# One fused attention and feed-forward kernel: the order of two early loads, chunk 1's queries and the second piece of `w_in`

## The chip, the cores and the metric

The kernel runs on one core of a Trainium2 chip. The core has TensorE (PE: matrix products; weight loads are listed apart as PEld), VectorE (DVE), ScalarE (ACT), GpSimd (POOL) and SyncE (SP, which here only issues transfers). Transfers between the chip's main memory and the on-chip memory run on 16 DMA engines that all queues share. The metric is the device time of one execution in microseconds (us). Six runs of the kernel before gave a median of 259.49 us, from 259.06 to 260.13.

## The reference, cut to what matters

Two blocks follow each other. The first is an attention with polynomial sketches: queries and keys are projected by two 8x32 matrices `S1` and `S2`, the 8x8 outer product of both projections gives 64 features, and the keys' features are summed up against the values.

```python
# q, k, v: (4, 4, 1088, 32);  S1, S2: (8, 32)
def phi(x):
    a = np.einsum('rd,bhsd->bhsr', S1, x)
    b = np.einsum('rd,bhsd->bhsr', S2, x)
    return np.einsum('bhsi,bhsj->bhsij', a, b).reshape(*x.shape[:-1], r * r)
q_p, k_p = (phi(q), phi(k))
kv = np.einsum('bhsf,bhsd->bhfd', k_p, v)
z = np.sum(k_p, axis=2)
num = np.einsum('bhsf,bhfd->bhsd', q_p, kv)
den = np.einsum('bhsf,bhf->bhs', q_p, z)[..., None] + 1e-06
attn_out = (num / den).astype(np.float32)

# x: attn_out as (4352, 128);  w_in: (128, 2048);  w_out: (2048, 128)
h = x @ w_in
g = 0.5 * h * (1.0 + erf(h * inv_sqrt2))
return (g @ w_out).astype(np.float32)
```

`w_in`, `w_out`, `S1` and `S2` arrive with 64-bit elements; the kernel loads both 32-bit words of each and rounds them to 32-bit floats on the chip.

## The kernel before, in words

The 1088 tokens of each of the 4 batches are cut into two chunks of 512 and a remainder of 64; the remainders of all batches form a ninth chunk. So chunk 0 and chunk 1 are the halves of batch 0. For each chunk the kernel makes `xT`, the attention output with its 128 channels on the partitions, then 16 hidden tiles (line 721, a product of `xT` with 128 columns of `w_in`, and Gelu at line 728), and sums them into the output with `w_out` (lines 807 and 858).

The weights are cut into five pieces of 256, 256, 512, 512 and 512 columns (`CUTS`, line 85), each a tile of its own: `w_in_sb[0]` serves hidden tiles 0 and 1, `w_in_sb[1]` hidden tiles 2 and 3. A piece lands in a raw tile (the pieces of 256 in tiles called `small`, those of 512 in tiles called `block`). The class `Rounding` (line 243) turns it into floats in steps: `low_words` (line 260, ScalarE), `exponent_fields` and `mantissa_fields` (lines 268 and 273, VectorE), `exponents` (line 279, ScalarE), `mantissas` (line 287, VectorE), `signs` (line 292, VectorE) and `product` (line 297, VectorE or POOL).

Every engine runs its instructions in the order of the text: at the end of the kernel a loop chains them (line 1219). SP's order is therefore that of the calls to the `load_` functions. It begins with batch 0's keys (line 192), chunk 0's queries (line 193), batch 0's values (line 195) and three remainders (line 197); then come `w_in`'s first piece, chunk 1's queries and `w_in`'s second piece (lines 198 to 200). The next entry on SP is the first piece of `w_out`, in `load_w_out` (line 175). It is gated: POOL writes one element of its landing tile (line 180), and the load waits for that write. POOL does it after the product of `w_in`'s first piece (lines 933 and 934). All remaining loads follow in `load_rest` (line 202).

How the loads in question are used, in the order of the text:

- Chunk 0's queries are turned by VectorE (line 528). Its features, the sums over keys and values (lines 426 and 432) and the rounding of `w_in`'s first piece follow.
- `query_turn(1, ...)` at line 928 turns chunk 1's queries with four TensorE transposes (line 333). ScalarE copies the result to `qT` at line 937; `expand_products(1)` (line 543) reads it.
- `w_in[1].low_words()` and `w_in[1].exponent_fields()` (lines 938 and 939) are the first readers of the second piece. Its other steps stand at lines 945, 951 and 955 to 957.
- Between them TensorE computes chunk 0's numerators by token (line 656, called at line 943), `expand_products(1)`, the transposes of chunk 0's attention output (line 694) and the first hidden tile (line 737). The other hidden tiles of chunk 0 follow at line 721.

At the very start, and once before the sketches, `keep_busy` (line 890) fills TensorE with products of zeros.

Of the kernel before, what the change touches and what calls it, by code (L numbers as in the profile page):

```python
# [16 lines left out]
def kernel(  # L17
# [97 lines left out]
    def load_q(n):  # L115
        at = n % NCH * CW
        if n < NCH:
            sp.dma_start(out=q_sb[n], in_=q[0, :, at:at + CW, :].rearrange("h (p j) d -> p h j d", j=JC))
            return
        for h in range(H):  # L120
            sp.dma_start(out=q_sb[n][h * 32:(h + 1) * 32].rearrange("t x j d -> t (x j d)"),
                         in_=q[n // NCH, h, at:at + CW, :].rearrange("(t n) d -> t (n d)", t=32))
# [8 lines left out]
    def load_rem(n, b):  # L131
        sp.dma_start(out=rem[n][b // 2 * REM:(b // 2 + 1) * REM, b % 2],
                     in_=src_of[n][b, :, MAIN:S, :].rearrange("h p d -> p h d"))
# [13 lines left out]
    def landing(dst, wide):  # L147

        if wide:
            rows, n = dst.shape  # L150
            if n == 512:

                if not half_block:
                    half_block.append(block())
                    r = half_block[0][:, 0:2]
                else:
                    r = half_block.pop()[:, 2:4]
                raw[dst.name] = r.rearrange("p a b -> p (a b)").rearrange("p (n two) -> p n two", two=2)
            elif n == 256:
                raw[dst.name] = small(U32).rearrange("p (n two) -> p n two", two=2)  # L160
            else:
                raw[dst.name] = big.tile([rows, n, 2], U32, name=f"raw_{dst.name}")
            return raw[dst.name].rearrange("p n two -> p (n two)")
        return dst

    def words(a):

        return (a, 1) if a.dtype == FP else (a.bitcast(U32), 2)

    def load_w_in(i):  # L170
        src, e = words(moe_w_in)
        c0, c1 = pieces[i]
        sp.dma_start(out=landing(w_in_sb[i], e == 2), in_=src[:, c0 * e:c1 * e])
# [22 lines left out]
    for n, b in (("k", 0), ("k", 2), ("v", 0)):  # L196
        load_rem(n, b)
    load_w_in(0)
    load_q(1)
    load_w_in(1)  # L200

    def load_rest():

# [1051 lines left out]
```

## Time and profile before

| what | value |
|---|---|
| median of six runs | 259.49 us (259.06 to 260.13) |
| the profiled execution's own time | 259.88 us |
| its span, first to last instruction | 258.1 us |
| granted TensorE clock over the span | 0.998 |
| TensorE matmul busy | 253.4 us, 98% of the span |
| VectorE, ScalarE, POOL busy | 151.1, 115.2, 164.1 us |
| read from and written to main memory | 10.88 MB, 2.23 MB |

The profile is of one execution, with times from the start of the span. "Busy" counts the time in which an engine has an instruction in execution; TensorE's matmuls overlap, and their ends are modelled, so that the start of one is firmer than its end. The chain that ended last is followed back from the last instruction, at each step to what released it; "issue" in it is time in which an engine waited for nothing that the profile shows. A DMA's time to landing runs from the start of its issue to the last of its 16 completion signals. The queues of kind "instruction" carry the program's own code.

### The profile page before, as it was taken

Reading aid. Unit: us, or ns where it says so; the run is one execution under the profiler, and the core shown is the slowest. Engines: PE = TensorE matmul, PEld = TensorE weight load, DVE = VectorE, ACT = ScalarE, POOL = GpSimd, SP = SyncE. Lnnn points to the kernel's source line nnn. Section 1 sums busy time; section 2 is a strip of 40 time slices with the busy share of each in tenths; the row PEclk is TensorE's granted clock in tenths of the full one; section 3 lists DMA queues with packets and bytes.
Section 4 is the critical chain, followed back from the end, with each engine's and each line's share of the span. In section 5 each row is a group of like instructions: output and inputs, shape, how many; then the busy total and the mean of one; then the engine's idle time right before and its main releaser. Section 6 shows DMA issues by size and latency. Waiting matters only on the chain.

```text
span 258.1 us, 5770 instructions
## 1 busy us (share of the span) xinstructions
PE 253.4 (98%) x2335; PEld 135.2 (52%) x2335; DVE 151.1 (59%) x313; ACT 115.2 (45%) x224; POOL 164.1 (64%) x173
## 2 busy tenths in 40 slices
PE   8899999999999999999999999999999999999995
PEld 7756444345444545544444455455444444445794
DVE  2886888969699997590187986399307000700330
ACT  4665777443626333443335332533444334433442
POOL 3504006799968778487758775787758777877300
PEclk9999999999999999999999999999999999999999
DMA  7489748810000101102000002000200200020020
GB/s 208 136 238 366 179 104 203 216 47 10 3 0 12 31 2 20 23 6 38 3 0 3 0 9 38 0 1 3 41 3 4 39 0 1 7 36 0 3 41 20
DMA packets 29594, 13.48 MB, mean 52 GB/s; under 512 B 21888, under 2 KB 27776, under 8 KB 29568
## 3 DMA queue, kind: packets, MB, share of 16 engines
q1 hardware_dynamic: 29392, 13.05, 20.4%
q8 instruction: 18, 0.29, 0.5%
q10 hardware_dynamic: 176, 0.07, 0.1%
q14 instruction: 8, 0.07, 0.1%
HBM read 10.88 MB, written 2.23 MB: 51 GB/s over the span
## 4 chain that ended last, share of the span: by engine, by line
PE 98%; issue 0%; ACT 0%
PE h_ps L721 45%; PE o_ps L807 33%; PE o_ps L858 5%; PE w_ps L855 3%; PE w_ps L437 1%; PE w_ps L578 1%; PE w_ps L633 1%; PE w_ps L890 1%; PE w_ps L543 1%; PE o_ps L426 1%; PE h_ps L737 1%; PE w_ps L978 1%; PE w_ps L656 0%; PE w_ps L333 0%; PE h_ps L333 0%
## 5 line engine op out<-in xcount | busy, mean ns | idle before, releaser
L721 PE MATMUL h_ps<-xT,w_in 128*64 128x512 f32 (+3 forms) x514 | 137.0, 576 | 0.0
L728 ACT ACTIVATE block<-h_ps 128x512 f32<-128x512 f32 (+1 forms) x128 | 73.1, 571 | 117.3 <-PE h_ps L721 115.3
L721 PEld LDWEIGHTS h_ps<-xT,w_in 128*64 128x64 f32 (+1 forms) x514 | 41.8, 142 | 30.6 <-issue 11.6
L807 PE MATMUL o_ps<-block,w_out 128*64 128x256 f32 x224 | 57.5, 379 | 0.0
L772 POOL TENSOR_TENSOR bits_low<-block 128x512 f32<-128x512 f32 x28 | 35.9, 1283 | 27.7 <-ACT block L728 27.7
L807 PEld LDWEIGHTS o_ps<-block,w_out 128*64 128x64 f32 x224 | 30.5, 137 | 38.1 <-issue 27.6
L773 POOL TENSOR_TENSOR bits_a<-block 128x512 f32<-128x512 f32 x28 | 35.8, 1278 | 11.9 <-ACT block L728 11.9
L822 DVE COPY sums<-o_ps 64x256 f32<-64x256 f32 x8 | 3.3, 417 | 60.7 <-PE o_ps L807 60.7
L774 POOL TENSOR_TENSOR bits_e<-bits_a,block 128x512 f32<-128x512 f32 x28 | 36.1, 1289 | 2.2
L775 POOL TENSOR_TENSOR bits_m<-block,bits_e 128x512 f32<-128x512 f32 x28 | 35.9, 1280 | 2.2
L807 PE MATMUL o_ps<-bits_a,small 128*64 128x256 f32 x112 | 28.8, 379 | 0.0
L807 PE MATMUL o_ps<-bits_low,small 128*64 128x256 f32 x112 | 28.8, 379 | 0.0
L807 PE MATMUL o_ps<-block,small 128*64 128x256 f32 x112 | 28.8, 379 | 0.0
L807 PE MATMUL o_ps<-bits_m,w_out 128*64 128x256 f32 x112 | 28.7, 379 | 0.0
L807 PEld LDWEIGHTS o_ps<-block,small 128*64 128x64 f32 x112 | 15.2, 137 | 17.9 <-issue 10.8
L807 PE MATMUL o_ps<-bits_e,small 128*64 128x256 f32 x112 | 17.0, 383 | 0.0
L858 PE MATMUL o_ps<-g,w_out 128*128 128x512 f32 (+1 forms) x34 | 16.5, 572 | 0.0
L807 PEld LDWEIGHTS o_ps<-bits_m,w_out 128*64 128x64 f32 x112 | 15.3, 137 | 0.0
L807 PEld LDWEIGHTS o_ps<-bits_a,small 128*64 128x64 f32 x112 | 15.2, 137 | 0.0
L807 PEld LDWEIGHTS o_ps<-bits_low,small 128*64 128x64 f32 x112 | 15.2, 137 | 0.0
L590 DVE STREAM_TRANSPOSE w_ps<-w_ps 128x512 f32<-128x512 f32 (+1 forms) x7 | 4.8, 688 | 17.0 <-ACT xT L644 12.7
L807 PEld LDWEIGHTS o_ps<-bits_e,small 128*64 128x64 f32 x112 | 7.6, 137 | 10.6 <-issue 8.8
(195 smaller groups left out, 304.1 us busy)
## 6 DMA issues: line engine op xcount, KB each, us to landing
block<-in_moe_w_in_dram SPq DMA_DIRECT2D x3, 512.0 KB, 7.6
block<-in_moe_w_out_dram SPq DMA_DIRECT2D x3, 512.0 KB, 11.3
k<-in_k_dram SPq DMA_DIRECT2D x12, 128.0 KB, 2.8
v<-in_v_dram SPq DMA_DIRECT2D x12, 128.0 KB, 3.3
q<-in_q_dram SPq DMA_DIRECT2D x24, 64.0 KB, 2.3
out_dram<-oT SPq DMA_DIRECT2D x21, 64.0 KB, 2.2
k<-in_k_dram SPq DMA_DIRECT2D x2, 256.0 KB, 3.3
q<-in_q_dram SPq DMA_DIRECT2D x2, 256.0 KB, 4.1
```

The source lines that it names most:

```text
L426: pe.matmul(ps[c * F:(c + 1) * F, r * 2 * D:r * 2 * D + C], lhsT=flat(k_p[0, r][:, t, c * 4 + ch * 2 + one]), rhs=v_aug[r][:, c, i, :C], s ...
L590: dve.transpose(out=tok, in_=ps[:, :, :H2])
L721: pe.matmul(ps[rows, :W], lhsT=w[:, rows], rhs=xT[n][:, :W], start=True, stop=True)
L728: act.activation(out=g_of[n, fi][:, :W], in_=ps[:, :W], func=ACT.Gelu)
L772: pool.tensor_sub(out=s[3], in0=a11, in1=a21)
L773: pool.tensor_add(out=s[1], in0=a21, in1=a22)
L774: pool.tensor_sub(out=s[2], in0=s[1], in1=a11)
L775: pool.tensor_sub(out=s[4], in0=a12, in1=s[2])
L807: pe.matmul(acc[n][bank][half * 64:(half + 1) * 64, col:col + HW], lhsT=fixed, rhs=moving, start=opens and e == 0 and name in "4715", stop ...
L822: dve.tensor_copy(out=N[lo, 0, one], in_=a0[lo, one])
L855: pe.matmul(o_of[n][i][:, :128], lhsT=g[:, i * 128:(i + 1) * 128], rhs=w_tile(w_out_sb, fi), start=first, stop=final)
L858: pe.matmul(o_of[n][:, cols], lhsT=w_tile(w_out_sb, fi), rhs=g[:, cols], start=first, stop=final)
```

## The change

The second piece of `w_in` is loaded ahead of chunk 1's queries, and not behind them. Nothing else is touched; the readers of both stand where they stood.

```diff
@@ -196,8 +196,8 @@
     for n, b in (("k", 0), ("k", 2), ("v", 0)):
         load_rem(n, b)
     load_w_in(0)
+    load_w_in(1)
     load_q(1)
-    load_w_in(1)
 
     def load_rest():
```

The two functions called, with `n` and `i` both 1:

```python
    def load_q(n):
        at = n % NCH * CW
        if n < NCH:
            sp.dma_start(out=q_sb[n], in_=q[0, :, at:at + CW, :].rearrange("h (p j) d -> p h j d", j=JC))
            return
...
    def load_w_in(i):
        src, e = words(moe_w_in)
        c0, c1 = pieces[i]
        sp.dma_start(out=landing(w_in_sb[i], e == 2), in_=src[:, c0 * e:c1 * e])
```

Each moves 256 KB: the queries as 512 rows of 512 bytes, the piece of `w_in` as 128 rows of 2,048 bytes.

## The prediction

> **What bounds the kernel now.** I read the page first, to see which engine carries the span, and in it the chain that ended last.
>
> ```profile
> span 258.1 us, 5770 instructions
> PE 253.4 (98%) x2335; PEld 135.2 (52%) x2335; DVE 151.1 (59%) x313; ACT 115.2 (45%) x224; POOL 164.1 (64%) x173
> PE 98%; issue 0%; ACT 0%
> ```
>
> TensorE is the chain from end to end. A change counts only if it opens or closes a gap between two of its instructions, or shortens them. So I next read the chain in order of time for the first 30 us, where both moved loads are used (start, length, what).
>
> ```profile
> 10.61 0.35 PE o_ps L432 x8
> 10.96 0.59 PE w_ps L333 x4
> 11.55 0.48 PE h_ps L656 x23
> 12.03 0.71 issue
> 12.74 0.32 PE h_ps L656 x9
> ```
>
> The four L333 pieces at 10.96 turn chunk 1's queries; they follow the sums before them without a gap. One line later is the only long gap of the start: 0.71 us at 12.03, in the middle of the chunk 0 numerators, put down to "issue" and to no semaphore. Third, the sync engine's timeline (start, length, queue and line, load), since the change is made there.
>
> ```profile
> 5.48 0.60 SPq L173 DMA_DIRECT2D small<-in_moe_w_in_dram  x1
> 6.13 0.43 SPq L118 DMA_DIRECT2D q<-in_q_dram  x1
> 6.61 0.50 SPq L173 DMA_DIRECT2D small<-in_moe_w_in_dram  x1
> 12.52 0.88 SPq L181 DMA_DIRECT2D small<-in_moe_w_out_dram  x2
> ```
>
> These are w_in's first piece, chunk 1's queries, w_in's second piece, and the gated loads behind them. Fourth, the two lines of the kernel by themselves, in the windows that hold only the second query load and only the second w_in load: issue to landing, the queries first; then the wait instruction that TensorE's sequencer executes before the turn.
>
> ```profile
> DMA to landing us min/median/max: 4.0/4.0/4.0
> ...
> DMA to landing us min/median/max: 4.3/4.3/4.3
> ...
> L333 PEldq EVENT_SEMAPHORE  x1: 51/51/51, 10.6 to 10.6; - x1
> ```
>
> So the queries land at 6.13 + 4.0 = 10.1 and w_in's second piece at 6.61 + 4.3 = 10.9. The wait at 10.6 ends at once; the list of waits has no line of TensorE on that load. Fifth, who reads the second piece, and what follows the turned queries (timelines of VectorE, ScalarE and TensorE).
>
> ```profile
> 11.58 0.29 DVE L268 TENSOR_SCALAR bits_e<-small 128x256 uint32<-128x256 uint32 x1
> ...
> 11.59 0.59 ACT L937 COPY qT<-w_ps 128x512 f32<-128x512 f32 x1 [0.35 <-PE w_ps L333]
> 12.07 0.43 ACT L260 ACTIVATE bits_low<-small 128x256 f32<-128x256 uint32 x1
> ...
> 13.46 1.12 PE L543 MATMUL w_ps<-qT,Srep 32*64 32x256 f32 x32
> ```
>
> None of these waits for the piece. Last, the DMA view from 10.4 to 10.6 us, which holds the end of all early loads: the columns are packets, MB and share of 16 engines.
>
> ```profile
> q8 instruction: 1, 0.02, 30.0%
> q1 hardware_dynamic: 1, 0.00, 0.3%
> ```
>
> One data packet ends the early loads, and one 16 KB packet of instructions starts there. 30% of 16 engines over 0.2 us is 0.96 us of one DMA engine. The same view from 10.6 to 13 us starts no packet at all. I read the 0.71 us gap as TensorE waiting for that block of code: it is in a group of 32 equal instructions, no semaphore ends it, and it is the first gap after the block arrives.
>
> **The change, part by part.**
>
> Removed and added: nothing. Two load instructions change places on the SP queue.
>
> The SP queue: w_in's second piece, 0.50 us of issue, passes the queries' 0.43 us. It is issued at 6.1 instead of 6.6, the queries at 6.1 + 0.5 = 6.6 instead of 6.1. The next instruction on SP, the gated load, goes at 12.52 after a wait of 5.4 us for POOL's memset; both issues are over by 7.1 either way. The memset follows POOL's product at 11.74, which waits for VectorE's signs at 11.24, made from the first piece, whose place is unchanged. So nothing behind on SP moves, and POOL's and ScalarE's own queues are passed by nothing: 0.
>
> w_in's second piece comes sooner. In the queries' old place it lands near 10.1 to 10.4 instead of 10.9. VectorE reads it first at 11.58, straight after the work in front of it in its order, ScalarE at 12.07: it had 0.7 us to spare already. TensorE needs it rounded at about 17.3 (third hidden tile), behind VectorE instructions that run without waiting for a load. Gain: 0. A gain is excluded because no reader waits.
>
> The queries come later. Both loads are 256 KB, so what is ahead of the last byte is the same in either order; I take for the queries the landing that the load in third place has now, 10.9. From below it is 6.61 + 4.0 = 10.6, if the queries keep their own time to landing; then nothing waits. From above, the block of code, which now starts when the data are through, gets in front of the last query packets on its DMA engine: 10.9 + 0.96 = 11.9. The middle value is the one nearest to the rows, because the code packet follows the last data packet in this trace and the number of packets ahead of it does not change.
>
> What that does to TensorE: its first L333 weight load starts at 10.89. A landing at 10.9 and a start just after it make a wait of about 0.1 us, at 11.0 (an estimate: the chunk 0 queries landed at 1.75 + 4.2 = 5.95, and VectorE began on them at 6.00). From below 0, from above 11.9 + 0.1 - 10.9 = 1.1 us. Behind the waiting instruction on TensorE stand the rest of the turn (0.59 us) and the numerators (0.48 us up to the gap). Those who wait for the turn: ScalarE's copy, 11.59 to 12.18, then at about 12.3; behind it the second piece's low words, 12.07 to about 12.2, not read before 15.9. TensorE uses the copy at 13.46, so 1.2 us are spare.
>
> The cover: the 0.1 us push the 23 numerators to end at 12.13 instead of 12.03, and the gap shrinks from 0.71 to 0.6. It ends at 12.74 as long as the code block leaves when it does now, and that packet starts at 10.5 behind the same bytes in either order. Path: +0.1 - 0.1 = 0. If that cover were gone the cost would be the whole wait, 0.1 and at most 1.1 us; with the cover the upper end is 1.1 - 0.71 = 0.4 us.
>
> [...]
>
> **Sum.** SP 0, second piece 0, queries +0.1, gap -0.1: 0.0 us. The profiled execution took 259.88 us, 1.78 outside its span; it lies 0.39 above the median of 259.49 of the six runs, and the change moves nothing that would carry that difference. I predict the median, rounded: 259.5 us. 0.2%, 0.52 us, is about what a measurement of this kernel can tell from no change.
>
> **Rivals.**
>
> Slower: the wait for the queries comes to lie on the path without its cover. Place: the four L333 turns at 10.89. The mechanism is the gap at 12.03 sliding along with the work before it. For it: the gap is labelled only "issue", and my reading of it as code is an inference. Against: no reason is visible why it should slide, since its packet starts at 10.5, before the wait. Price: the whole wait, 0.1 to 1.1 us, middle 0.6: 260.1 us, at most 260.6. It decides from a wait of 0.52 us, that is, from a landing of the queries at about 11.3.
>
> Faster: the code block overtakes the query packets, and the gap goes while the queries are not late. For it: the queries' many small rows now come last, and a packet that slips between them would start before 10.5. Against: on its DMA engine it occupies 0.96 us, by which the queries are then late, so the 0.71 us gained at 12.03 are lost at 10.9. Both would have to be true. Price: up to -0.71, 258.8 us.
>
> No effect by another road: the loads share the DMA engines so closely that both land as before. For it: issues 0.5 us apart and landings 0.8 apart. Price 0, 259.5 us; it ends with the forecast.
>
> Later stall: the turned queries reach TensorE late at 13.46. Against: 1.2 us spare against 0.1; even the upper end of 1.1 fits. 259.5 us.
>
> **How the numbers follow.** Forecast with the two rivals that end on it, path unchanged or moved within 0.52 us: 0.70. Slower rival: 0.22, of which I let all count as slower. Faster rival: 0.08. The range covers the forecast's own spread, 259.1 to 260.1 as the runs before lie, and reaches up to 260.4, over most of the slower rival, and down to 258.9, short of the faster one's end.
>
> **What would show it.** Right: w_in's second piece issued before the queries near 6.1; the queries landing near 10.9; the first L333 of chunk 1 at 10.9 to 11.1; the gap in L656 shortened to about 0.6 and ending near 12.7; the rest of the chain at its old times. Wrong: a line of TensorE waiting for the query load longer than 0.5 us; the gap ending later than 12.9, or gone; the instruction packet starting at another time than 10.5; the first L737 away from 15.3. The prediction fails if the gap is not tied to that packet, or if the order changes when the packet leaves.

## The result, and the profile after

The kernel after takes 259.86 us (median of 36 runs, 259.13 to 262.07), the kernel before 259.39 us (median of 74 runs). The ratio is 1.0019 with a 95% interval of 1.0011 to 1.0027: slower by 0.47 us, just within the 0.2% that the prediction set as its bound, but clear of no change. The profiled execution after took 259.90 us with a span of 258.1 us, the same span as that of the profiled execution before. So the two profiles shown first do not contain the difference; further executions were needed.

The page of the kernel after: its span, the engines' busy time, and the shares of the chain that ended last.

```profile
span 258.1 us, 5770 instructions
PE 253.3 (98%) x2335; PEld 135.6 (53%) x2335; DVE 151.1 (59%) x313; ACT 115.1 (45%) x224; POOL 164.0 (64%) x173
PE 94%; SPq 2%; DMA 2%; issue 0%; ACT 0%
```

The instructions are the same. What is new is 2% of DMA in a chain that was all TensorE. The chain in order of time (start, length, what) shows where:

```profile
6.12 0.43 SPq L173
6.55 0.04 issue
6.60 5.12 DMA q<-in_q_dram
11.71 0.14 issue
11.85 0.63 PE w_ps L333 x4
12.48 0.60 PE h_ps L656 x32
13.08 0.47 PE o_ps L656 x32
```

The order on SP is as the change says: `w_in`'s second piece at 6.12, chunk 1's queries at 6.60. But the queries take 5.1 us and land at 11.71, and TensorE cannot turn them before 11.85, where before it had started at 10.96 in this chain. And the 0.71 us gap at 12.03 is gone: the 32 numerators run in one piece, and the next products begin at 13.08, against 13.06 before. A wait of 0.8 us has come and a gap of 0.7 us has gone, in this pair of executions. The list of waits after, from 5 to 25 us (who waited for what: us in total, times, longest):

```profile
PE w_ps L333 <- DMA q<-in_q_dram: 0.8, 1, 0.8
ACT bits_low L260 <- DMA small<-in_moe_w_in_dram: 0.4, 1, 0.4
```

The second line is the first piece of `w_in`, which lands at 10.35; TensorE does not wait for it in this execution. The DMA view after, from 8.8 to 8.9 us, shows what has changed ahead of both (packets, MB, share of 16 engines):

```profile
q8 instruction: 1, 0.02, 82.5%
q1 hardware_dynamic: 19, 0.02, 59.4%
```

TensorE's 16 KB block of code leaves here, at 8.85 us, in the middle of the data, where it left at 10.48 in the profile before, behind all of them. (That queue q8 carries TensorE's code is my reading: the page of before gives it 18 packets and 0.29 MB, and TensorE 4,670 matmuls and weight loads, some 260 for each packet.) The trace gives each of a load's 16 completion signals. Of the queries' signals after, eleven come by 10.26, the other five between 10.51 and 11.71.

The trace also has the start and length of each packet, but not its engine. Where one packet starts as another ends and the rest follow without a break, I take them to be on one engine. By this the queries behind the code block run from 10.16 to 11.33. But a second engine, which has rows of `w_in`'s second piece until 10.67, runs its queries until 11.44. So in this execution the block is one of two causes of the late landing, and without it the queries would have been about as late.

### The profile page after: what moved, and what is told of

It reads as the page before. It is cut to its first block, busy times and chain, and to the rows that moved or that the text cites. A ratio compares the mean times of both kernels' runs of the same rounds, so it can differ in the third digit from the quotient of the medians.

```text
span 258.1 us, 5770 instructions
## 1 busy us (share of the span) xinstructions
PE 253.3 (98%) x2335; PEld 135.6 (53%) x2335; DVE 151.1 (59%) x313; ACT 115.1 (45%) x224; POOL 164.0 (64%) x173
## 4 chain that ended last, share of the span: by engine, by line
PE 94%; SPq 2%; DMA 2%; issue 0%; ACT 0%
PE h_ps L721 45%; PE o_ps L807 33%; PE o_ps L858 5%; PE w_ps L855 3%; DMA q<-in_q_dram 2%; PE w_ps L437 1%; PE w_ps L578 1%; PE w_ps L633 1%; PE h_ps L737 1%; SPq L132 1%; SPq L100 1%; PE w_ps L978 1%; PE w_ps L656 0%; PE w_ps L543 0%; SPq L173 0%; PE w_ps L333 0%
## 5 line engine op out<-in xcount | busy, mean ns | idle before, releaser
L773 POOL TENSOR_TENSOR bits_a<-block 128x512 f32<-128x512 f32 x28 | 35.7, 1276 | 12.0 <-ACT block L728 11.9
L807 PEld LDWEIGHTS o_ps<-bits_e,small 128*64 128x64 f32 x112 | 7.7, 137 | 10.6 <-issue 8.8
```

Source lines behind the costliest of these rows:

```text
L773: pool.tensor_add(out=s[1], in0=a21, in1=a22)
L807: pe.matmul(acc[n][bank][half * 64:(half + 1) * 64, col:col + HW], lhsT=fixed, rhs=moving, start=opens and e == 0 and name in "4715", stop ...
```

## The experiments

Fourteen executions were profiled in all. I tell two theories apart. A: the order of the two loads decides when the code block leaves, so that each order has its own profile. B: the block leaves early or late by the execution, and in either order it gets in front of whichever load stands third on its DMA engine; in before that load is one with time to spare, in after it is the one that TensorE waits for.

### Both kernels once more: look_before, look_after

Edit: none. `look_before` is the kernel before, `look_after` the kernel after.

> The kernel before, unchanged, looked at once more. Two theories. Theory A (order): in the order of before the block of code leaves behind both loads, near 10.5 us, and TensorE has the gap of about 0.7 us at 12.0; in the order of after it leaves in front of the queries, near 8.9, the gap is gone, and the queries land near 11.7. By A this look repeats the first: code at 10.4 to 10.6, a gap of 0.6 to 0.8 us in L656, no wait at L333. Theory B (chance): when the code leaves differs from execution to execution, whatever the order of the two loads. By B this look may as well show the code near 9 us, no gap at 12.0 and the first L333 at 10.9 to 11.1; then before is usually faster than its first profile by the gap.

> The kernel after, unchanged, once more, timed against before. Both theories expect the time at 1.001 to 1.003 of before. A: the profile repeats itself, with the code near 8.9 us, a wait of TensorE of 0.8 to 0.9 us for the query load and no gap at 12.0. B: the code may leave near 10.5; then the queries land near 10.9, the first L333 stands near 11.0, and the gap of 0.6 us is there.

Measured: `look_before` 258.9 us, span 257.1. `look_after` 259.8 us, 1.0017 of before (1.0002 to 1.0031), span 258.2. The chain of `look_before` around the place:

```profile
10.54 0.35 PE o_ps L432 x8
10.89 0.59 PE w_ps L333 x4
11.48 0.60 PE h_ps L656 x32
12.08 0.47 PE o_ps L656 x32
12.55 1.05 PE w_ps L543 x32
```

No gap: all 32 numerators run through, and the next products begin at 12.08, 1 us earlier than in the first profile of before. Its DMA view from 8 to 10.4 us has the instruction packet that the first profile of before had at 10.48 (start 8.79 by the trace):

```profile
q1 hardware_dynamic: 658, 0.52, 65.7%
q8 instruction: 1, 0.02, 2.9%
```

Here the third load, `w_in`'s second piece, pays for it: it lands at 6.6 + 4.8 = 11.4, and nobody waits for it. In `look_after` the third load is the queries; of their 16 signals fifteen come by 10.45, the last at 11.81:

```profile
11.81 0.14 issue
11.95 0.63 PE w_ps L333 x4
12.58 0.60 PE h_ps L656 x32
```

In this trace the first row behind the block starts at 10.28, as the block ends at 10.29, and from 10.4 on the packets follow one another on that engine alone: this landing is the block's doing.

Theory A falls: before has the early block too. These two executions fit theory B, and the account below limits it. The gap that I had counted on as cover is not in every execution.

### Chunk 1's queries first: q_first

```diff
-    load_w_in(0)
     load_q(1)
+    load_w_in(0)
     load_w_in(1)
```

> Chunk 1's queries are loaded ahead of both pieces of w_in. If the loss of after is TensorE's wait for the queries, this order has no such wait (queries landing near 9.5): time at or below before, 0.998 to 1.000, with the gap at 12.0 of 0 to 0.8 us depending on when the code leaves. w_in's first piece lands about 0.7 us later than in before, near 10.1 to 10.4; VectorE reads it at 10.3, so at most 0.3 us of VectorE's spare time is used. If the loss of after were something else than the queries' landing (the two w_in pieces back to back, for instance, which this order has too), this one would lose about 0.2% as well.

Measured: 0.9998 of before (0.9988 to 1.0007). The interval lies below that of after, 1.0011 to 1.0027. The two pieces of `w_in` stand back to back here too, without the loss of after, so that neighbourhood is not the cause. The queries come in time; in their place the first piece is late, at 10.6, and ScalarE waits for it (list of waits of `q_first`):

```profile
ACT bits_low L260 <- DMA small<-in_moe_w_in_dram: 0.7, 1, 0.7
```

By the table below this costs 0.2 us, since the sums' copy stands behind that instruction on ScalarE and TensorE's numerators wait for it. The expectation put the first piece at 10.1 to 10.4 and the cost at spare time of VectorE alone; it did not see ScalarE's order.

### The second piece out of the early queue: w1_gated

```diff
-    def load_w_in(i):
+    def load_w_in(i, gated=False):
...
-        sp.dma_start(out=landing(w_in_sb[i], e == 2), in_=src[:, c0 * e:c1 * e])
+        to = landing(w_in_sb[i], e == 2)
+        if gated:
+            pool.memset(to[0:1, 0:1], 0)
+        sp.dma_start(out=to, in_=src[:, c0 * e:c1 * e])
...
     load_w_in(0)
     load_q(1)
-    load_w_in(1)
...
     widen_v(0)
+    load_w_in(1, gated=True)
```

> w_in's second piece is taken out of the early queue: its load waits for a one-element write of POOL behind the first widening of the values, near 7.4 us, and so is issued near 7.5 and not at 6.6, behind the queries. If the DMA backlog ahead of the code block makes the gap at 12.0, the block leaves about 0.6 us earlier than 10.5 (eight rows of 2 KB at 0.08 us fewer ahead of it on its DMA engine), and the gap shrinks to 0.1 or goes; the queries still land near 10.1 and TensorE does not wait for them: 0.997 to 0.999 of before. If the gap is not tied to that packet it stays at about 0.7 us, and the time is that of before, 0.999 to 1.001. The second piece then lands near 11.5 to 12, still before ScalarE's and VectorE's next use at 13.

Measured: 1.0001 of before (0.9991 to 1.0011). Its profile has the code at 8.90, the queries at 10.3, the second piece at 11.4 and no gap and no wait between the sums and the first hidden tile. The gain of 0.1 to 0.3% that I expected did not come, and by theory B little of it could: the late block with its long gap, which it guards against, is in one of five executions of before.

### More executions, and less or more in front of the queries: look_before2, look_after2, w1_half, q_gated

`look_before2` and `look_after2` are before and after, unchanged. The edit of `w1_half`, against after:

```diff
-        sp.dma_start(out=landing(w_in_sb[i], e == 2), in_=src[:, c0 * e:c1 * e])
+        to = landing(w_in_sb[i], e == 2)
+        m = (c1 - c0) * e // (2 if i == 1 else 1)
+        sp.dma_start(out=to[:, :m], in_=src[:, c0 * e:c0 * e + m])
...
     for t in v_aug:
         dve.memset(t[:, :, :, D:C], 1.0)
+    dve.memset(raw[w_in_sb[1].name].rearrange("p n two -> p (n two)")[:, 256:], 0)
```

The edit of `q_gated`, against after:

```diff
     load_w_in(0)
     load_w_in(1)
-    load_q(1)
...
     widen_v(0)
+    pool.memset(q_sb[1][0:1, 0, 0, 0:1], 0.0)
+    load_q(1)
```

> A third look at before, to see how often the gap at 12.0 us is there. Of two looks one had it (code block leaving at 10.5, span 258.1) and one had not (code at 8.8, no gap, span 257.1). If the code usually leaves early, this look has the code near 9, the first L333 at 10.9 to 11.2, no gap of over 0.3 us after it, and a span of 257.1 to 257.5. The span should be the start of the first L737 plus 242.7 us, as in all six profiles so far.

> A third look at after. In two of two the code left near 9 and the queries landed at 11.7 and 11.8. If that is the usual course, this look shows them at 11.2 to 11.9 and a wait of TensorE of 0.4 to 1.0 us; span again the start of the first L737 plus 242.7. If the wait were an accident of those two executions, the queries land near 10.9 and the wait is 0.1.

> The order of after, but w_in's second piece loads only its first 128 columns; VectorE fills the other half of the landing tile with zeros at the start, so hidden tile 3 is left without its weights. The queries then have four rows of 2 KB fewer ahead of them on each DMA engine, 0.32 us at 0.08 each. If the queries' landing at 11.7 is the data ahead plus the code block on one DMA engine, they land near 11.4 and TensorE waits about 0.6 instead of 0.9 us; time 0.9985 to 1.001 of before, 0.3 us below after. If bytes ahead do not matter, 11.7 and the time of after, 1.002.

> The order of after, with the queries held back further: their load waits for a one-element write of POOL behind the first widening of the values, near 7.4 us, and is issued 0.8 to 1.0 us later than in after. If the queries' landing sets TensorE's start at L333 one for one, and they are behind the code block already, they land 0.0 to 0.5 us later (11.7 to 12.3), TensorE waits 0.9 to 1.5 us and the time is 1.002 to 1.005 of before. If the late landing in after were only the later issue, the wait would grow by the whole 0.8 to 1.0 us, to 1.7 to 2.0, and the time to 1.006. If the wait at L333 did not pass through to the end, the time stays at 1.002 with a longer wait.

Measured: `look_before2` 259.27 us, `look_after2` 259.82 us, `w1_half` 1.0013 of before (1.0003 to 1.0023), `q_gated` 1.0020 (1.0008 to 1.0032).

`look_after2` repeats the late queries, at 11.63. `look_before2` shows that the order of before is not free either. Its second piece lands at 12.05, and the list of waits of that execution has

```profile
DVE bits_e L268 <- DMA small<-in_moe_w_in_dram: 0.5, 1, 0.5
```

VectorE stands at the exponent fields of that piece while the numerators it should divide are ready, and TensorE later stands idle for 0.17 us until VectorE has divided them (line 694).

That is not the whole loss of 0.25 us in this execution. TensorE's lines for the 32 numerators, first in `look_before`, then in `look_before2`:

```profile
11.41 0.67 PE L656 MATMUL h_ps<-kz,q_pT 64*64 64x33 f32 x32
```

```profile
11.44 0.85 PE L656 MATMUL h_ps<-kz,q_pT 64*64 64x33 f32 x32
```

The 0.18 us more lie between the 23rd and the 24th matmul, where the first profile of before has its gap. The 24th starts 1.30 us after the end of the code packet in the first profile of before and 1.40 us after it here. In the other twelve executions it starts 1.7 us or more after that end, and there is no gap. Without VectorE's wait `look_before2` would still lose some 0.17 us (an estimate: 0.17 us of idle time less in front of line 694, and 0.33 us from there to the first hidden tile, as in `look_before`).

`w1_half` puts the queries at 6.6 + 4.5 = 11.1, 0.5 to 0.7 us earlier than the first three executions of after (I expected 0.3). TensorE does not wait for them, the turn following the last sums at 11.30, and yet the time did not come down to the 0.9985 to 1.001 that I expected. It lies between before and after, but the interval holds after's 1.0019 too, so only the landing is shown, and that in one execution. That it is the smaller load which moves it is not shown either: the last query packet ends at 10.29, and the last signal comes 0.85 us after it, against 0.27 to 0.41 us in the four executions of after. (The halved piece still goes as 128 rows, of 1 KB each; my expectation counted half as many of 2 KB.)

In `q_gated` the queries are issued at 7.54, 0.94 us later than in after, and land at 11.52, no later than in the first three executions of after (11.63 to 11.81). TensorE's line in the timeline, with the idle time before it and its releaser (line 332 there is line 333 of before):

```profile
11.65 0.63 PE L332 MATMUL w_ps<-ident,q 128*128 128x128 f32 x4 [1.07 <-DMA q<-in_q_dram]
```

So an issue 0.94 us later did not make the landing later, in this one execution. The rows behind the code block are again the last of all; they run until 11.16. The wait is longest here only because the sums end earliest, as the table shows.

### Taking the wait away, and the last executions: other_q, look_before3, look_before4, look_after3

The edit of `other_q`, against after, in `query_turn`:

```diff
-[q_sb[1][:, h].rearrange("p j d -> p (j d)") for h in range(H)]
+[q_sb[0][:, h].rearrange("p j d -> p (j d)") for h in range(H)]
```

> The order of after, every load as in after, but TensorE's four turns at L333 read chunk 0's queries, which landed at 6 us, in place of chunk 1's: chunk 1's results are left out. Nothing then waits for the third load. If TensorE's wait for the queries is the whole loss of after, the first L333 is back at 10.9 to 11.2, no gap of over 0.3 us follows (the code block leaves near 9), the second piece of w_in has landed by 9.8 so that VectorE does not wait for it either, and the time is at or below before: 0.998 to 1.000. If the loss of after were in the two w_in pieces back to back or in the code block's own place, the time stays at 1.0015 to 1.002.

> A fourth look at before. The three so far paid 0.98 us (late code: the gap at 12.0), 0 and 0.36 us (VectorE waits for w_in's second piece, landed at 12.05) against the best start of L737, 14.38. Expected: again the code near 9 with the second piece landing at 11.3 to 12.1, and L737 at 14.4 to 14.8; a late code block at 10.5 with L737 at 15.4 if that is more than one execution in four.

> A fifth look at before, with the same expectation as the fourth: L737 at 14.4 to 14.8, or 15.4 when the code block leaves late; span L737 plus 242.7.

> A fourth look at after. The three so far waited 0.58 to 0.97 us for the queries, L737 at 15.29 to 15.48. Expected: the queries landing at 11.5 to 11.9 and L737 at 15.2 to 15.5; if the code block leaves behind the queries here, a landing near 10.9, L333 near 11.0, a gap in or near L656 and L737 near 15.4.

Measured: `other_q` 259.49 us against 259.44, ratio 1.0012 with a wide interval of 0.9994 to 1.0030. That lies between the 0.998 to 1.000 that I expected and the 1.0015 to 1.002 of the other case, and the interval holds 1.000 as well as 1.002: the time does not decide. In its profile the wait is gone, the turn following the sums at once, but at 11.39 and not at 10.9 to 11.2, because the sums are late. `look_before3` 259.72 us, `look_before4` 259.40, `look_after3` 259.82.

`look_before4` is as expected. `look_before3` is not: its second piece lands at 10.43, before the code block, which left at 9.59, is through, and its first hidden tile stands at 15.12 with nothing lost, since TensorE comes late to the last sums.

`look_after3` does not show the wait that I expected: the queries land at 11.3, and TensorE is not ready for them before 11.7. Its timeline, and that of `look_before3`, which is late in the same way without any load to wait for:

```profile
11.37 0.42 PE L432 MATMUL o_ps<-v_rem_aug,k_p_rem 128*64 128x33 f32 x8
11.73 0.66 PE L333 MATMUL w_ps<-ident,q 128*128 128x128 f32 x4
```

```profile
11.29 0.43 PE L432 MATMUL o_ps<-v_rem_aug,k_p_rem 128*64 128x33 f32 x8
11.64 0.66 PE L333 MATMUL w_ps<-ident,q 128*128 128x128 f32 x4
```

### The account of fourteen executions

From each trace: the start of the code packet, the landing of the third early load, and the first matmul of the last sums (L432 in before), of the turn (L333) and of the first hidden tile (L737), all in us by TensorE's timeline. "Lost" is the time from L432 to L737 above 3.83 us, the least that occurs.

| execution | code leaves | third load lands | last sums | turn | first hidden tile | lost | span |
|---|---|---|---|---|---|---|---|
| before, first profile | 10.48 | w_in 10.86 | 10.54 | 10.89 | 15.28 | 0.91 | 258.1 |
| look_before | 8.79 | w_in 11.39 | 10.47 | 10.82 | 14.30 | 0.00 | 257.1 |
| look_before2 | 9.60 | w_in 12.05 | 10.50 | 10.85 | 14.58 | 0.25 | 257.5 |
| look_before3 | 9.59 | w_in 10.43 | 11.29 | 11.64 | 15.12 | 0.00 | 257.9 |
| look_before4 | 9.45 | w_in 11.54 | 10.96 | 11.32 | 14.80 | 0.01 | 257.6 |
| after, first profile | 8.85 | queries 11.71 | 10.60 | 11.85 | 15.30 | 0.87 | 258.1 |
| look_after | 9.08 | queries 11.81 | 10.55 | 11.95 | 15.40 | 1.02 | 258.2 |
| look_after2 | 9.34 | queries 11.63 | 10.76 | 11.76 | 15.21 | 0.62 | 258.0 |
| look_after3 | 9.46 | queries 11.30 | 11.37 | 11.73 | 15.21 | 0.01 | 258.0 |
| q_first | 8.98 | w_in 11.61 | 10.47 | 10.82 | 14.50 | 0.20 | 257.3 |
| w1_gated | 8.90 | w_in 11.35 | 10.69 | 11.04 | 14.52 | 0.00 | 257.3 |
| w1_half | 9.15 | queries 11.14 | 10.94 | 11.30 | 14.77 | 0.00 | 257.8 |
| q_gated | 9.04 | queries 11.52 | 10.16 | 11.65 | 15.10 | 1.11 | 257.9 |
| other_q | 9.62 | queries 11.33 | 11.04 | 11.39 | 14.87 | 0.00 | 257.7 |

From the first hidden tile to the end it is 242.8 or 242.9 us in every row but `w1_half`, where it is 243.0. So in these executions the whole difference between the kernels arises before 15.4 us. In the rows where the queries stand third and TensorE reads them, the turn starts at the later of two times: 0.35 to 0.36 us after the last sums begin, or 0.13 to 0.15 us after the landing.

How much of the late landings is the code block's doing? In ten of the fourteen executions rows of the third load follow behind it on its engine. In the first profile of before it left last of all. In `look_before3`, `look_after3` and `other_q` no packet starts behind it. In the last two the queries still land at 11.30 and 11.33, on an engine that carried no block; in `look_after3` that engine had rows of `w_in` until 10.26. So theory B is true of most executions but is not the whole: the third load can be late without the block, and why one engine falls behind the others there is open.

The mean loss is (0.91 + 0.00 + 0.25 + 0.00 + 0.01) / 5 = 0.23 us in the five executions of before and (0.87 + 1.02 + 0.62 + 0.01) / 4 = 0.63 in the four of after. The difference, 0.40 us, is near the 0.47 between the medians. Nine executions are few for such means; that the account closes is a consistency, not a measurement of its own.

## Why the prediction held in its number and failed in its steps

The predicted time was 259.5 us within 258.9 to 260.4, most likely no change; measured was 259.86. By its steps:

- The SP queue, cost 0: right. The issues stand at 6.12 and 6.60, and the gated load at 12.60, against 12.52 before.
- `w_in`'s second piece, gain 0 because no reader waits: right for the execution that I read. In `look_before2` VectorE does wait for it, some 0.08 us of the path by the estimate above, which the order of after removes. A gain was not excluded, only small.
- The queries' landing, taken as 10.9: wrong. They land at 11.3 to 11.8 in the four executions of after. I had this as the upper end, 11.9, with its mechanism, the code block in front of the last query packets with 0.96 us, and took the other end because one trace had the block behind all data. In thirteen of fourteen executions it leaves before 9.7 us. This mechanism alone sets the landing in two of the four (`look_after`, `look_after2`); in the first profile of after a second engine is as late, and in `look_after3` the block has no part in it. The 10.9 was one draw too: the third load of before lands at 10.43 to 12.05 in five executions.
- The wait at the turn, 0.1 us: mis-sized for the same reason. It is 0.58, 0.83 and 0.97 us in three executions and nothing in the fourth.
- The cover, the 0.71 us gap at 12.03: the step that failed most. It is no property of the kernel, but depends on how late the block comes: it takes 0.91 us of the path in the first profile of before, 0.18 us in `look_before2`, and is absent in the other three executions of before and all four of after. Where there is no gap there is no cover. That the gap is a wait for code, as I read it, is supported: both gaps lie at the same matmul and end 1.3 to 1.4 us after the code packet, and in no other execution does TensorE get there so soon after it. No run moved the packet on purpose.
- The rivals: the slower one, the wait at the turn without its cover, is what happened, by another road than I gave: the gap does not slide, it is not there. Its price, 0.6 us in the middle, compares with 0.40 by the account and 0.47 measured. The faster rival's first half, the block overtaking the queries, also happened in three of the four executions of after, and the queries paid for it as the text said.

The number held by luck. The sum of zero rests on a cover that is mostly not there. Two things that the sum did not have shrink the wait of 0.6 to 1.0 us: TensorE is itself late in some executions, so that the landing is hidden, and before has losses of its own. The range holds the result because it was drawn over most of the slower rival.

TensorE's first 16 KB packet leaves in every execution after some 260 to 370 of its matmuls and weight loads, and in two there was a gap after about 440. In the other twelve there was none.

## What to carry to other kernels

One profile shows one draw of everything that races at the start. Before a gap is booked as cover, check that a second execution has it. In a queue of early loads the last one is exposed to whatever holds up one of the 16 DMA engines, here most often a 16 KB block of code that takes 0.96 to 1.32 us of one: the last place belongs to the load whose reader has that much time to spare. With TensorE as the reader the wait was 0.58 to 0.97 us in three of four executions of after; with VectorE it cost some 0.08 us, by the estimate above, in one of five of before.

## What the runs showed of the hardware

In `look_after` the queries were as late as their slowest DMA engine: fifteen of their sixteen completion signals were there by 10.45 us, the sixteenth came at 11.81, by my reading of the packets on an engine that carried the code packet from 9.08 to 10.29. The block costs its engine more than its own 0.96 to 1.32 us: in `look_before` the first three rows of 2 KB behind it take 0.23 us each, where most take 0.08.

The time at which TensorE reaches the last sums differs by 1.2 us, from 10.16 to 11.37, between the fourteen executions, in which TensorE's instructions up to there are the same. Much of it is in the first products. In `look_before` and in `look_before3` the key turns of line 361 read (duration in ns, minimum, median and maximum; first and last start):

```profile
L361 PE MATMUL h_ps<-ident,k x2: 272/300/328, 4.9 to 5.1; 128*128 128x128 f32 x2
```

```profile
L361 PE MATMUL h_ps<-ident,k x2: 422/448/475, 5.4 to 5.7; 128*128 128x128 f32 x2
```

The same matmul takes 272 ns or 422 ns, and the change from slow to fast falls between 3.8 us (in `q_gated`) and 6.4 us (in `look_after3`); in `look_before3` the last of these turns, at 6.1 us, is still slow. The starts of these turns lie 0.21 us apart in `look_before3` and 0.11 us in `look_before`. The granted clock of both executions reads 1.00 in every stretch from 0 to 8 us, so that view does not show it. What makes the matmuls slow, and why the change comes at another time in each execution, no run here shows.
